# Strassen blocks in three of the four quarters of the mixed group's first product, and residual-only results on ScalarE and GpSimd

## The chip, the cores and the metric

The kernel runs on one core of a Trainium2 chip. Its time is the device time of one execution in microseconds; the time before is the median of three runs. The engines are TensorE (PE in the profile; PEld is its weight load), VectorE (DVE), ScalarE (ACT), GpSimd (POOL) and SyncE (SP, which issues transfers).

## The reference, cut to what matters

Attention with exponential features on both signs, then a normalised two-layer product with a residual:

```python
# attention: batch 8, heads 8, seq 576, head_dim 64, 128 features
def phi(x):
    proj = x @ w_phi; proj = proj - max(abs(proj))
    return concat([exp(proj), exp(-proj)])
kv = phi(k).T @ v ;  z = sum(phi(k));  attn = (phi(q) @ kv) / (phi(q) @ z + 1e-6)
# the rest: 8 x 576 tokens of 512
xn = (x - mean) / sqrt(var + 1e-6) * g_ln
out = x + max(xn @ w_ch1, 0) @ w_ch2        # 512 -> 2048 -> 512
```

All 4608 tokens go through both products. Only these two products, and of them the end, are touched by the change.

## The kernel before, in words

The tokens of the second part are worked in nine groups of 512 (`NM` = 4 tiles of 128 tokens). Groups 0 to 6 are ordinary ones, group 7 (`MIX`) holds the tokens that are left over from every sequence, group 8 (`LAST`) is the last. For a group the first product makes `hT`, 2048 hidden rows in 16 steps `jj` of 128 (`first`, L1425): four matmuls of 512 columns each and a relu. The second product, followed by the residual, makes `o` and stores it. Four steps `jj` are a quarter.

Groups 6, 7 and 8 (`FAST`) do the second product with Strassen's seven products for each pair `p` of token tiles (`fast`, L1541). It has two chains of accumulators, `ch`, and seven results; each is scaled by `rstd` and added to `o`. Four of the seven are "fresh": they are the first to write their piece of `o` and add the residual `x` instead of an older `o`. In group 7 the two chains lie in one tile of two banks, in group 6 and 8 in tiles of their own.

Group 8 does the first product by Strassen as well, group 7 in one quarter of four (`QUICK`, L533). A Strassen quarter (`quick`, L1744) has seven products of four matmuls with 256 columns. They go to three accumulators: name 1 is the single bank `n_bank`, names 0 and 2 are chains that several products are added to. A chain is read between its products: `sum_` on VectorE adds a copy of another chain to it and writes `hT`; `keep` copies a chain to SBUF for a later `sum_`; a relu ends it. The weights' sums (`F`, in the buffers `b_0`, `b_1`, `b_2`, `qkT_141` to `qkT_143` and `v_101`) and the tokens' sums (`X`, in `ea` and `eb`) are made by VectorE before.

The order of all engines is written out when the kernel is built, by a planner (`Order.run`, L365). It takes every operation with an assumed duration and with the keys that it reads and writes, and gives an engine that is free the waiting operation with the lowest rank. An operation that may run on two engines goes to the one that takes it first. `latest` (L374) works due times back from an operation's users. The ranks of the attention come from these. On the chip every engine works its own queue in that order and waits by semaphores, which the framework sets by the tiles that instructions read and write. The planner's keys don't set them.

Of the kernel before, what the change touches and what calls it, by code (L numbers as in the profile page):

```python
# [10 lines left out]
FP32 = mybir.dt.float32  # L11
BF16 = mybir.dt.bfloat16
AF = mybir.ActivationFunctionType
# [283 lines left out]
class Op:  # L297
    __slots__ = (
        "engines", "engine", "us", "emit", "rank", "lag", "deps", "users", "acquire", "release",
        "ready", "left", "number", "due", "load", "cut", "last",  # L300
    )
# [25 lines left out]
class Order:  # L327
# [5 lines left out]

    def add(self, engine, us, rank, emit, r=(), w=(), acquire=None, release=None, lag=None, due=None, load=None, cut=None, last=False):
        op = Op()
        op.last = last
# [28 lines left out]
    def run(self):  # L365
# [23 lines left out]
        while events:  # L389
# [12 lines left out]
            for engine, queue in waiting.items():  # L402
# [54 lines left out]
                elif isinstance(us, Turn):  # L457
                    ahead = backlog["DMA"]
                    if free["DMA_w"] > now:
                        ahead *= 3.4  # L460
                    us = max(us.us, max(0.0, free["DMA"] - now) + ahead - 0.5)
                elif isinstance(us, Op):
                    us = 1.1 if us.engine == "ACT" else 0.0
                if engine == "POOL" and op.load is None:
# [26 lines left out]
def kernel(  # L491
# [40 lines left out]
    FAST = (LAST - 2, LAST - 1, LAST)  # L532
    QUICK = {LAST: range(4), MIX: (2,)}  # L533
    LEAD = 24
    CP = JC // 2
    FH = DM // 2
# [1004 lines left out]
    def fast(g, p, i, cs):  # L1541
# [59 lines left out]

        def result():
# [3 lines left out]
            nc.vector.scalar_tensor_tensor(  # L1606
                out=o, in0=sums(), scalar=rstd_x[:, g, t : t + 1],
# [76 lines left out]
    def sums_of_w1(gate):  # L1684
# [3 lines left out]
        for i in range(2):  # L1688
            for home_ in (b16_home[i], qkT_home[i]):
                add("SP", 0.0, RELU, None, w=[*home_, (home_[0], "free")])  # L1690
        for home_ in (b16_home[2], qkT_home[2], v_home, *U_home, *W_home, *Y_home):
            add("SP", 0.0, RELU, None, w=[*home_, (home_[0], "free")])
        for half in range(2):
# [8 lines left out]
            for i in (0, 1, 3, 2):  # L1702
                a, b, op_, reads = todo[i]

                def emit(k, out_=F_of[half][i], a=block(a), b=block(b), op_=op_):
                    nc.vector.tensor_tensor(out=out_[:, k], in0=a[:, k], in1=b[:, k], op=op_)

                for k in range(2):
                    add("DVE", Port(0.32), 2000.0 + half, lambda k=k, f=emit: f(k),
                        r=[("w1", n_, kc) for n_ in range(2 * half, 2 * half + 2) for kc in range(KC)]  # L1710
                        + [("F", half, j, k) for j in reads] + [(F_at[half][i][1][0], "free"), *gate],
                        w=[("F", half, i, k)])

    def sums_of_x(g):
# [9 lines left out]

        add("SP", 0.0, RELU, None, w=[*X_home[g], ("X home", g)])
        todo = ((X1, block(0, 1), block(0, 0), ()), (X2, block(1, 1), own(X1), (0,)),
                (X3, block(1, 1), block(0, 1), ()), (X4, block(1, 0), own(X2), (1,)))
        for i in range(4):
            out_, a, b, reads = todo[i]

            def emit(k, out_=own(out_), a=a, b=b):
                nc.vector.tensor_tensor(out=out_[:, k], in0=a[:, k], in1=b[:, k], op=ALU.subtract)

            for k in range(2):
                add("DVE", Port(0.2), RELU if g == LAST else 2001.0, lambda k=k, f=emit: f(k),
                    r=[("xT", g % XB, kc) for kc in range(KC)] + [("X", g, j, k) for j in reads]
                    + [("X home", g)], w=[("X", g, i, k)])

# [5 lines left out]
    def quick(g, d):  # L1744
# [26 lines left out]
        def products(name, left, right, start, stop, r, w=(), acquire=None):  # L1771
            def emit():
                if start:
                    st[name] = (
                        n_bank[:, 0 : 2 * FH] if name == 1
                        else ps_B.tile([P, 2 * FH], FP32, tag="B", name="sum")
                    ).rearrange("p (c t) -> p c t", c=2)
# [6 lines left out]

            add("PE", mm(4, FH), turn_of(g), emit, r=r, w=[("quick", g, d, name), *w], acquire=acquire,
                due=due(g, 4 * d / JC) + (0.0 if start and name < 2 else 40.0))
# [21 lines left out]
        def keep(name):  # L1808
            def emit(engine):
                kept(name)  # L1810
                if engine == "DVE":
                    nc.vector.tensor_copy(out=st["kept", name], in_=st[name])
                else:
                    nc.scalar.copy(out=st["kept", name], in_=st[name])
# [14 lines left out]
        X = [[("X", g, i, k) for k in range(2)] for i in range(4)]  # L1829
        def sum_(odd_, t, name, other, w, release=None):  # L1830
            add("DVE", 0.66, RELU,
                both(ring_at(odd_, t), lambda: st[name], lambda: st["kept", other]),
                r=[q_key(name), ("kept", other, d % 2)], w=w, release=release)

        products(1, A(0, 1), B(1, 0), True, True, w_keys + x_keys, acquire=("N", 1))
        yield
        keep(1)
        products(0, A(0, 0), B(0, 0), True, True, w_keys + x_keys, acquire=("B", 1))
        yield
        sum_(0, 0, 0, 1, even)  # L1840
        products(2, S(0), T(0), True, True, F[0] + X[0], acquire=("B", 1))
        yield
# [9 lines left out]
        add(("ACT", "DVE"), (0.55, 0.6), RELU, relu(ring_at(1, 0), lambda: st[0]),  # L1852
            r=[q_key(0)], w=odd, release=("B", 1))
        products(2, S(3), B(1, 1), False, True, F[3] + x_keys)
        yield
        sum_(0, 1, 2, 0, even, release=("B", 1))
# [26 lines left out]
    def moe(g):  # L1883
# [5 lines left out]
        if g == LAST:  # L1889
            quick_moe(g)  # L1890
            return
        quicks = None
        if QUICK.get(g):
            sums_of_w1([("S", p, 2, SH) for p in range(2)])
            sums_of_x(g)
            quicks = quick(g, QUICK[g][0])
        for jj in range(JC):
            if g <= LAST and jj // 4 not in QUICK.get(g, ()):
                if quicks and jj >= JC - 4:
                    for _ in range(2):  # L1900
                        next(quicks, None)
# [202 lines left out]
```

## Time and profile before

| what | value |
|---|---|
| median of 3 runs | 356.84 us (356.49 to 356.98) |
| profiled execution | 356.53 us |
| its span | 354.7 us |
| TensorE busy | 346.6 us (98%) |
| VectorE busy | 302.5 us (85%) |
| ScalarE busy | 257.9 us (73%) |
| GpSimd busy | 196.5 us (55%) |

A row of a group of instructions gives line, engine, operation, tiles written and read, shapes, count, then busy time and mean duration of one in ns, then the idle time before them and who ended it. A row of the timeline gives start, duration, engine, line, operation, tiles and count. A row of the chain of waits gives start and length of a piece of the chain that ended last. Times are counted from the start of the span.

### The profile page before, as it was taken

How to read it: one execution, taken by the hardware profiler on the slowest of the kernel's cores; microseconds unless marked ns; L12 is line 12 of the kernel's file. 1: busy time of each engine (PE TensorE's matmuls, PEld its weight loads, DVE VectorE, ACT ScalarE, POOL GpSimd, SP SyncE). 2: the span in 40 equal slices, each digit the busy share in tenths (PEclk: the TensorE clock that was granted, in tenths of full speed). 3: DMA queues.
4: the chain of work that ended last, by engine and by line, in shares of the span. 5: the costliest groups of instructions: out<-in, count | busy, mean ns of one | idle time of the engine just before them, and what ended most of it. 6: DMA issues, size and time to landing. Idle time of an engine off the chain costs nothing.

```text
span 354.7 us, 9383 instructions
## 1 busy us (share of the span) xinstructions
PE 346.6 (98%) x3615; PEld 221.7 (62%) x3640; DVE 302.5 (85%) x659; ACT 257.9 (73%) x553; POOL 196.5 (55%) x249
## 2 busy tenths in 40 slices
PE   8999999999999999999999999999999999999995
PEld 8988855556554555454545555555555578578884
DVE  5699989799998888878889899887778799999983
ACT  4998977598988897969696875887697833656410
POOL 5389756596765876648579698565546411000000
PEclk9999999999999999999999999999999999999999
DMA  8999999999997878389629542851051004500053
GB/s 212 325 197 269 205 260 270 243 245 239 292 250 205 208 184 224 104 168 252 201 69 178 103 110 41 150 156 35 2 126 63 3 9 115 124 0 3 0 120 118
DMA packets 93676, 53.89 MB, mean 152 GB/s; under 512 B 61104, under 2 KB 88048, under 8 KB 93632
## 3 DMA queue, kind: packets, MB, share of 16 engines
q1 hardware_dynamic: 89392, 47.72, 56.3%
q0 software_dynamic: 3328, 4.49, 7.4%
q10 hardware_dynamic: 912, 1.08, 1.0%
q8 instruction: 28, 0.46, 0.5%
q14 instruction: 16, 0.13, 0.1%
HBM read 36.77 MB, written 9.44 MB: 130 GB/s over the span
## 4 chain that ended last, share of the span: by engine, by line
PE 87%; DVE 7%; ACT 4%; issue 1%; POOL 0%; DVEq 0%
PE hT_ps L1431 29%; PE ch_ps L1463 23%; PE ch L1597 9%; PE pm L990 4%; PE n_bank L1141 4%; PE sum L1780 4%; PE num L1199 3%; PE n_bank L2064 3%; ACT ea L1111 2%; PE pt L999 2%; PE n_bank L1135 1%; DVE numc L1221 1%; DVE m L1047 1%; DVE numc L1227 1%; PE n_bank L1199 1%
## 5 line engine op out<-in xcount | busy, mean ns | idle before, releaser
L1431 PE MATMUL hT_ps<-xT,w 128*128 128x512 bf16 x496 | 119.5, 379 | 0.1
L1463 PE MATMUL ch_ps<-w,hT 128*128 128x512 bf16 x363 | 89.3, 379 | 1.3 <-issue 0.3
L1047 DVE TENSOR_REDUCE m<-pm 128x8 f32<-128x1024 f32 x64 | 77.0, 1216 | 8.1 <-PE pm L990 6.4
L1074 POOL TENSOR_TENSOR vv<-v,ek 128x1024 bf16<-128x1024 f32 x32 | 61.0, 1907 | 37.9 <-issue 21.3
L1431 PEld LDWEIGHTS <-w 128*128 128x128 bf16 x496 | 43.9, 98 | 43.2 <-issue 1.3
L1067 ACT ACTIVATE eb<-pm 128x1024 bf16<-128x1024 f32 x64 | 65.0, 1039 | 4.4 <-DVE m L1047 4.4
L1111 ACT ACTIVATE ea<-pt 128x1024 bf16<-128x1024 f32 x64 | 64.1, 1039 | 3.5 <-PE pt L999 2.7
L1441 ACT ACTIVATE hT<-hT_ps 128x512 bf16<-128x512 f32 x73 | 43.7, 599 | 24.9 <-PE hT_ps L1431 24.1
L1266 POOL TENSOR_TENSOR x<-numc,rden 128x128 bf16<-128x128 f32 (+1 forms) x64 | 39.1, 614 | 39.9 <-DVE rden L1233 37.9
L1463 PEld LDWEIGHTS <-hT 128*128 128x128 bf16 x384 | 34.0, 98 | 34.3 <-issue 0.8
L1439 DVE TENSOR_SCALAR hT<-hT_ps 128x512 bf16<-128x512 f32 x51 | 34.8, 685 | 8.4 <-PE hT_ps L1431 8.0
L1199 PEld LDWEIGHTS <-ea 128*128 128x128 bf16 x512 | 24.6, 97 | 9.9 <-issue 0.7
L902 POOL TENSOR_TENSOR b<-qk,one 128x1024 bf16<-128x1024 f32 x14 | 26.9, 1927 | 4.7 <-DMA qkT<-b 3.0
L1141 PE MATMUL n_bank<-vv,eb 128*128 128x65 bf16 x512 | 26.7, 194 | 0.0
L2064 PE MATMUL n_bank<-wz 128*128 128x120 bf16 x355 | 25.5, 226 | 0.1
L1141 PEld LDWEIGHTS <-eb 128*128 128x128 bf16 x512 | 22.3, 98 | 4.5
L1338 DVE BATCH_NORM_STATS2 st<-x 128x6 f32<-128x512 bf16 (+1 forms) x40 | 21.8, 572 | 1.7 <-POOL x L1266 1.4
L2064 PEld LDWEIGHTS <-wz 128*128 128x128 bf16 x355 | 22.2, 104 | 1.1
L1480 POOL TENSOR_TENSOR o<-o,x 128x512 f32<-128x512 f32 x15 | 17.4, 1157 | 10.1 <-ACT o L1476 9.9
L1221 DVE TENSOR_TENSOR numc<-num,em 128x390 f32<-128x390 f32 (+1 forms) x40 | 20.4, 515 | 2.7 <-PE num L1205 1.6
L1227 DVE TENSOR_TENSOR numc<-numc,num 128x390 f32<-128x390 f32 (+1 forms) x40 | 20.5, 517 | 0.5
L1476 ACT ACTIVATE o<-ch_ps,rstd 128x512 f32<-128x512 f32 x15 | 10.3, 686 | 14.3 <-PE ch_ps L1463 14.3
(162 smaller groups left out, 618.4 us busy)
## 6 DMA issues: line engine op xcount, KB each, us to landing
out_dram<-o SPq DMA_DIRECT2D x29, 256.0 KB, 2.4
qk<-in_k_dram SPq DMA_DIRECT2D x12, 512.0 KB, 5.4
qk<-in_q_dram SPq DMA_DIRECT2D x12, 512.0 KB, 6.4
v<-in_v_dram SPq DMA_DIRECT2D x12, 512.0 KB, 4.7
w<-in_moe_w_ch_dram POOLq DMA_DIRECT2D x4, 1024.0 KB, 11.3
qk<-in_k_dram SPq DMA_DIRECT2D x8, 256.0 KB, 6.8
qk<-in_q_dram SPq DMA_DIRECT2D x7, 256.0 KB, 7.1
v<-in_v_dram SPq DMA_DIRECT2D x7, 256.0 KB, 7.6
```

What stands on the lines that cost most here:

```text
L1047: nc.vector.reduce_max(out=m, in_=ps, axis=AX.X, apply_absolute_value=True)
L1067: nc.scalar.activation(eb, ps, AF.Exp, scale=(1.0, -1.0)[t])
L1074: eng.tensor_tensor(out=u["vv"][:, :, 0:MX, 0:D], in0=bcast(vb[:, hh, :].rearrange("p (c d) -> p c d", d=D), 1, 2), in1=bcast(e[:, :, 0:MX ...
L1111: nc.scalar.activation(u["EA"][:, t, 0:1024], u["pt"], AF.Exp, scale=(1.0, -1.0)[t])
L1141: nc.tensor.matmul(ps[:, t, c // 4, :], EB[:, t, c, :], vv[:, t, c, :], start=False, stop=(t == 0 and c == MX - 1), skip_group_check=True,)
L1199: nc.tensor.matmul(ps[t][:, i, :], ea(u, t, c), KV[:, t, c // 4, :], start=True, stop=True,)
L1266: eng.tensor_tensor(out=dst, in0=src, in1=by, op=ALU.mult)
L1431: nc.tensor.matmul(st["ps"], w1_sb[:, kc, jj * P : (jj + 1) * P], xT_bufs[g % XB][:, kc::KC, :], start=(kc == 0), stop=(kc == KC - 1),)
L1439: nc.vector.tensor_relu(h_sb, st["ps"])
L1441: nc.scalar.activation(h_sb, st["ps"], AF.Relu)
L1463: nc.tensor.matmul(ch[g, i], hT[g, jj][:, i * P : (i + 1) * P], w2_sb[:, jj, :], start=(jj == 0), stop=(jj == JC - 1),)
L2064: nc.tensor.matmul(warm, wz, wz[:, 0:WN], start=False, stop=False, skip_group_check=True)
```

## The change

`QUICK` gives group 7 quarters 1, 2 and 3 to Strassen in place of quarter 2 alone. The two chains of such a quarter, names 0 and 2, no longer take a bank each from the pool `ps_B`. They share one tile of two banks, `sum2`, from `ps_A`. All three quarters are put to the planner at their own place, in place of one that was spread over the last steps. The copies and two of the closing relus, which could go to VectorE or ScalarE, are ScalarE's alone. A fresh result of groups 6 and 7 may go to ScalarE, which scales it into `o`; GpSimd then adds the residual. Users marked `calm` no longer count when due times are worked back. What is computed stays the same.

```diff
-    QUICK = {LAST: range(4), MIX: (2,)}
+    QUICK = {LAST: range(4), MIX: (1, 2, 3)}
+    EITHER = lambda g, i: g != LAST
...
-            late = min((latest[o.number] for o in op.users), default=1000.0) - op.lag
+            late = min((latest[o.number] for o in op.users if not o.calm), default=1000.0) - op.lag
...
# fast(): results
+            if engine == "ACT":
+                nc.scalar.activation(o, sums(), AF.Copy, scale=rstd_x[:, g, t : t + 1])
+                return
...
-        add("DVE", 0.44, RELU, result, r=[("fast", g, p, bank)],
-            w=o_key + ([counts["slot", g, t]] if i in (0, 3) else []),
-            release=gave)
+        either = fresh and EITHER(g, i)
+        op = add(
+            ("DVE", "ACT") if either else ("DVE",), (0.44, 0.46)[: 1 + either], RELU,
+            result if either else lambda: result("DVE"), r=[("fast", g, p, bank)], w=w, release=gave,
+        )
+        if either:
+            def residual():
+                if op.engine == "ACT":
+                    o = ch["o", g, t][:, f]
+                    nc.gpsimd.tensor_tensor(
+                        out=o, in0=o, in1=token_tile(g, t)[2][:, f], op=ALU.add
+                    )
+            add("POOL", op, RELU, residual, r=[], w=o_key, cut=0.6)
...
# quick(): the chains
+                    if g == MIX and name == 0:
+                        st["A"] = ps_A.tile([P, 2, 2 * FH], FP32, tag="A", name="sum2")
                     st[name] = (
                         n_bank[:, 0 : 2 * FH] if name == 1
+                        else st["A"][:, name // 2, :] if g == MIX
                         else ps_B.tile([P, 2 * FH], FP32, tag="B", name="sum")
...
-            add(("ACT", "DVE"), (0.55, 0.6), RELU, emit, r=[q_key(name), (home_, "free")],
-                w=[("kept", name, d % 2)], release=("N", 1) if name == 1 else None)
+            add("ACT", 0.55, RELU, emit, r=[q_key(name), (home_, "free")],
+                w=[("kept", name, d % 2)], calm=True, release=("N", 1) if name == 1 else None)
...
-        add(("ACT", "DVE"), (0.95, Port(0.4)), RELU, relu(wide_, lambda: wide_), w=even)
-        add(("ACT", "DVE"), (0.55, Port(0.25)), RELU, relu(ring_at(1, 1), lambda: ring_at(1, 1)), w=odd)
+        add("ACT", 0.95, RELU, lambda f=relu(wide_, lambda: wide_): f("ACT"), w=even, calm=True)
+        add("ACT", 0.55, RELU, lambda f=relu(ring_at(1, 1), lambda: ring_at(1, 1)): f("ACT"), w=odd, calm=True)
...
# moe(): where the quarters are put to the planner
-            quicks = quick(g, QUICK[g][0])
...
+                for _ in quick(g, jj // 4):
+                    pass
```

The order is the same on every engine up to about the start of group 7's first product. Three places differ in what matters here. In the rows below `sum_5505`, `sum_5514` and `sum_5633` are the two-bank tiles of quarters 1, 2 and 3 of group 7 and `sum` is a chain in a bank of its own; `xT_139` are group 7's tokens and `xT_140` group 8's; what stands in brackets are the engines whose semaphores a row waits for. Of a product's four matmuls the first is shown.

First, TensorE at the start of Strassen's products in group 7. Before:

```order
L1780 MATMUL n_bank<-xT_139,w_132 128x256
...
L1780 MATMUL sum<-xT_139,w_132 128x256 [waits Activation_49]
...
L1431 MATMUL hT_ps<-xT_139,w_132 128x512 [waits Activation_49]
...
L1780 MATMUL sum<-ea_125,qkT_141 128x256 [waits Activation_49]
...
L1597 MATMUL ch_5556<-w_133,hT 128x256
...
L1780 MATMUL sum<-ea_125,qkT_142 128x256 [waits DVE_49]
...
L1780 MATMUL sum<-xT_139,qkT_143 128x256 [waits DVE_49]
```

Now:

```order
L1803 MATMUL n_bank<-xT_139,w_132 128x256
...
L1803 MATMUL sum_5505<-xT_139,w_132 128x256 [waits DVE_49]
...
L1803 MATMUL sum_5514<-xT_139,w_132 128x256
...
L1803 MATMUL sum_5505<-ea_125,b_0_145 128x256 [waits DVE_49]
...
L1803 MATMUL n_bank<-xT_139,w_132 128x256 [waits Activation_49]
...
L1803 MATMUL sum_5514<-ea_125,qkT_141 128x256
...
L1803 MATMUL sum_5505<-ea_125,b_1_146 128x256 [waits Activation_49]
...
L1803 MATMUL sum_5505<-xT_139,b_2_147 128x256
...
L1803 MATMUL n_bank<-xT_139,w_132 128x256 [waits Activation_49]
...
L1803 MATMUL sum_5514<-xT_139,qkT_143 128x256 [waits DVE_49]
```

and ScalarE and VectorE with it, now (ScalarE's rows first):

```order
L1834 COPY kept<-n_bank 128x512 [waits PE_49]
L1834 COPY vx_107<-sum_5505 128x512 [waits DVE_49]
L1834 COPY kept<-n_bank 128x512 [waits PE_49]
L1834 COPY vx_106<-sum_5514 128x512 [waits PE_49]
L1834 COPY qx_89<-sum_5505 128x512 [waits PE_49]
...
L1820 TENSOR_TENSOR hT<-sum_5505,kept 128x2x256 [waits PE_49,Activation_49]
L1752 TENSOR_TENSOR eb_148<-xT_139,ea_125 128x256 [waits DVE_49] x2
L1820 TENSOR_TENSOR hT<-sum_5514,kept 128x2x256 [waits Activation_49]
```

Before, wide matmuls of `hT_ps` and products of `ch` stood between the products of one quarter; now products of two quarters alternate, each with its two chains in one tile.

Second, TensorE in quarter 3 of group 7, which before was worked in wide matmuls of `hT_ps`. Now:

```order
L1803 MATMUL sum_5633<-xT_139,w_132 128x256 [waits DVE_49]
...
L1803 MATMUL sum_5633<-ea_125,qkT_141 128x256
...
L1600 MATMUL ch_5645<-w_133,hT 128x256 [waits PE_49]
...
L1803 MATMUL sum_5633<-ea_125,qkT_142 128x256 [waits DVE_49]
...
L1803 MATMUL sum_5633<-xT_139,qkT_143 128x256 [waits Activation_49]
...
L1803 MATMUL sum<-ea_127,v_101 128x256 [waits Activation_49]
...
L1803 MATMUL sum_5633<-ea_125,v_101 128x256 [waits Activation_49]
...
L1803 MATMUL sum<-eb_149,w_132 128x256 [waits DVE_49]
L1803 MATMUL sum_5633<-eb_148,w_132 128x256 [waits DVE_49]
```

Three products of this quarter now wait, one of them directly behind a product that it shares the tile with.

Third, VectorE around 295 us, with the results of group 6 (`o<-ch`) and the first weight sums. Before:

```order
L1233 RECIPROCAL rden<-numc 128x6
L1706 TENSOR_TENSOR b_0_145<-w_132 128x512
L1606 SCALAR_TENSOR_TENSOR o<-ch_5291,rstd,x 128x256
L1706 TENSOR_TENSOR b_0_145<-w_132 128x512
L1606 SCALAR_TENSOR_TENSOR o<-ch_5303,rstd,x 128x256
L1606 SCALAR_TENSOR_TENSOR o<-ch_5282,rstd,o 128x256
L1338 BN_STATS st<-x 128x6
```

Now, and behind the dots the end of GpSimd's queue:

```order
L1236 RECIPROCAL rden<-numc 128x6
L1612 SCALAR_TENSOR_TENSOR o<-ch_5303,rstd,o 128x256
L1725 TENSOR_TENSOR b_0_145<-w_132 128x512 x2
L1341 BN_STATS st<-x 128x6 x2
L1612 SCALAR_TENSOR_TENSOR o<-ch_5282,rstd,o 128x256
...
L1269 TENSOR_TENSOR x<-numc,rden 128x2x3x64
L1646 TENSOR_TENSOR o<-o,x 128x256 x2
L1269 TENSOR_TENSOR x<-numc,rden 128x2x3x64
L1646 TENSOR_TENSOR o<-o,x 128x256 x5
L1646 TENSOR_TENSOR o<-o,xm 128x256 x7
```

Fourteen of the sixteen fresh results of groups 6 and 7 left VectorE; the weight sums moved up, and fourteen adds stand at the end of GpSimd's queue.

More of the change, by code (lines that the diff above doesn't have):

```diff
@@ L299 @@
         "engines", "engine", "us", "emit", "rank", "lag", "deps", "users", "acquire", "release",
-        "ready", "left", "number", "due", "load", "cut", "last",
+        "ready", "left", "number", "due", "load", "cut", "last", "calm",
     )
@@ L462, in run @@
                 elif isinstance(us, Op):
-                    us = 1.1 if us.engine == "ACT" else 0.0
+                    us = (op.cut or 1.1) if us.engine == "ACT" else 0.0
                 if engine == "POOL" and op.load is None:
@@ L1600, in products, with result @@
                 )
-        def result():
+        def result(engine):
             if i in (0, 3):
@@ L1783, in emit @@
                         )
-            add("PE", mm(4, FH), turn_of(g), emit, r=r, w=[("quick", g, d, name), *w], acquire=acquire,
+            add("PE", mm(4, FH), turn_of(g), emit, calm=not (start and name < 2), r=r, w=[("quick", g, d, name), *w], acquire=acquire,
                 due=due(g, 4 * d / JC) + (0.0 if start and name < 2 else 40.0))
@@ L1808, in keep, with emit @@
         def keep(name):
-            def emit(engine):
+            def emit():
                 kept(name)
[L1811 to L1814, printed above, removed]
+                nc.scalar.copy(out=st["kept", name], in_=st[name])
             home_ = (U_home, Y_home, W_home)[name][d % 2][0]
-            add(("ACT", "DVE"), (0.55, 0.6), RELU, emit, r=[q_key(name), (home_, "free")],
-                w=[("kept", name, d % 2)], release=("N", 1) if name == 1 else None)
+            add("ACT", 0.55, RELU, emit, r=[q_key(name), (home_, "free")],
+                w=[("kept", name, d % 2)], calm=True, release=("N", 1) if name == 1 else None)
         def relu(out_, in_):
@@ L1891, in moe @@
             return
-        quicks = None
         if QUICK.get(g):
-            sums_of_w1([("S", p, 2, SH) for p in range(2)])
+            sums_of_w1([("S", p, 0, SH) for p in range(2)])
             sums_of_x(g)
-            quicks = quick(g, QUICK[g][0])
         for jj in range(JC):
             if g <= LAST and jj // 4 not in QUICK.get(g, ()):
-                if quicks and jj >= JC - 4:
-                    for _ in range(2):
-                        next(quicks, None)
                 first(g, jj)
```

44 lines of the change are left out of this document (25 added, 19 removed).

## The prediction

> **What bounds the kernel now.** I read the shares first, then the tail of the program in slices of ten microseconds, then the waits of TensorE, then the chain of waits.
>
> ```profile
> span 354.7 us, 9383 instructions
> PE 346.6 (98%) x3615; PEld 221.7 (62%) x3640; DVE 302.5 (85%) x659; ACT 257.9 (73%) x553; POOL 196.5 (55%) x249
> ...
> 290.00:300.00 10.00, 9.77 (x90) 8.62 (x89) 9.98 (x29) 2.37 (x5) 0.90 (x1) 1.00 0.29 54
> 300.00:310.00 10.00, 10.00 (x59) 5.49 (x58) 9.31 (x31) 6.43 (x13) 0.00 (x0) 1.00 0.59 159
> 310.00:320.00 10.00, 10.00 (x82) 7.83 (x80) 9.71 (x27) 5.73 (x11) 0.00 (x0) 1.00 0.00 0
> 320.00:330.00 10.00, 10.00 (x94) 8.96 (x92) 8.59 (x20) 6.08 (x10) 0.00 (x0) 1.00 0.01 2
> ...
> PE ch L1597 <- DVE o L1606: 0.2, 1, 0.2
> PE ch_ps L1463 <- issue: 0.2, 1, 0.2
> ...
> 292.83 8.02 PE ch L1597 x72
> 300.86 6.91 PE hT_ps L1431 x32
> ...
> 337.85 13.11 PE ch L1597 x120
> 350.96 0.03 issue
> ```
>
> The columns of the slices are stretch, length, then busy time of TensorE, weight loads, VectorE, ScalarE and GpSimd, and the granted clock (1.00). After 240 us TensorE waits 0.4 us in all, and from 292.83 to 350.96 it runs without a gap. So the end of the program is TensorE's work in this stretch, plus whatever it waits; the 3.7 us behind 350.96 (last result, store) do not change. VectorE is at 9.98, 9.31 and 9.71 of 10 us in the stretch that the change rewrites: it bounds nothing yet, but has little slack. ScalarE and GpSimd are light there. The order on every engine is the same up to about 290 us, so only what follows counts.
>
> **Work taken from TensorE.** 32 matmuls of 512 columns take 6.91 us, 0.216 each; 120 of 256 columns take 13.11 us, 0.109 each. A plain quarter has 16 of the former, 3.46 us, a Strassen quarter 28 of the latter, 3.06 us (seven products of four, 0.437 each). Two more quarters: **-0.79 us**. The sums of weights and tokens that Strassen needs were made before too, so they add nothing.
>
> The 0.2 us that TensorE waits for `o` at 292.8 belongs to a result which now goes to ScalarE, idle there: **-0.20** (bounds -0.35, with the refill below, and 0).
>
> **Waits put into TensorE's queue.** Before, each Strassen chain had its own bank; now both chains of a MIX quarter lie in one tile, and the order shows the waits. ScalarE's copy of the second half (`vx_107<-sum_5505`) waits for VectorE, though TensorE wrote that half; and the next product into the first half (`sum_5505<-ea_125,b_1_146`) waits for ScalarE, though VectorE read that half. So sum and copy, which could run side by side, stand behind one another, with TensorE behind both. Their prices:
>
> ```profile
> L1797 DVE TENSOR_TENSOR hT<-sum,kept 128x512 bf16<-128x512 f32 x3 | 2.1, 686 | 0.1
> L1814 ACT COPY vx<-sum 128x512 f32<-128x512 f32 x3 | 1.8, 585 | 0.2 <-PE sum L1780 0.2
> ...
> 317.54 0.68 DVE L1797 TENSOR_TENSOR hT<-sum,kept 128x512 bf16<-128x512 f32 x1
> 318.28 0.59 ACT L1814 COPY qx<-sum 128x512 f32<-128x512 f32 x1 [1.50 <-DVE hT L1797]
> 332.71 0.58 ACT L1814 COPY vx<-sum 128x512 f32<-128x512 f32 x1
> 333.19 0.59 ACT L1814 COPY qx<-sum 128x512 f32<-128x512 f32 x1
> ```
>
> A sum takes 0.69, a copy 0.59; copies in a row start 0.49 apart (332.71, 333.19); from VectorE's end (317.54 + 0.68) to ScalarE's start 0.06, so I take 0.05 for each hand-over. When TensorE starts again it loses about 0.15: the 72 matmuls after the gap at 292.83 took 8.02 us, against 72 x 0.109 = 7.87.
>
> Place 1, quarter 1 of MIX. Count from the end of its `n_bank` product. Its copy `kept` ends at 0.69 (0.05, about 0.05 behind the last relu, 0.59). TensorE makes three products, to 1.31; the third writes the second half of `sum_5505`, and VectorE's sum waits for that too: 1.36 to 2.05. The copy `vx_107` follows, 2.10 to 2.69, and TensorE may go on at 2.74. In between it has two products, to 2.19: **0.55 us of waiting**.
> Place 2, quarter 2. ScalarE starts its next two copies at 2.59 and 3.08 and ends the latter, `vx_106`, at 3.67; the sum of `sum_5514` runs 3.72 to 4.41; TensorE needs it at 4.46. It came on at 2.74, lost 0.15, and did three products, to 4.20: **0.26**.
> Place 3, quarter 3. Count from the end of the first sum of `sum_5633`. TensorE makes `sum_5633<-ea_125,qkT_142`, 0.05 to 0.49; the copy `vx_107` comes behind this write, 0.54 to 1.13; and directly behind in TensorE's queue stands `sum_5633<-xT_139,qkT_143`, which waits for the copy, to 1.18: **0.69**.
> Place 4, same quarter. That product ends at 1.18 + 0.15 + 0.44 = 1.77, the copy `qx_89` at 2.41, TensorE goes on at 2.46; one product in between, to 2.21: **0.25**.
> Together 1.75, and four refills, 0.60: **+2.35**. In the other quarters, the last group's, each chain keeps its own bank. Two rows of the same kind stand further on (`sum_5633<-eb_148` and a `sum<-eb_149`, both behind a sum of VectorE): 0 to 0.69 each; I take 0.05 each and the refills, **+0.40**, nearer to nothing since other products stand ahead of them.
> For the four the bounds are 0 (if the waits named are met early) and 3.4 (four sums of 0.69 in full, four refills).
>
> **Results on ScalarE and GpSimd.** Seven residual-only results of group 6 and seven of MIX leave VectorE, and GpSimd adds the residual.
>
> ```profile
> L1606 DVE SCALAR_TENSOR_TENSOR o<-ch,rstd,x 128x256 f32<-128x256 f32 x16 | 7.7, 479 | 1.7 <-PE ch L1597 1.6
> L1476 ACT ACTIVATE o<-ch_ps,rstd 128x512 f32<-128x512 f32 x15 | 10.3, 686 | 14.3 <-PE ch_ps L1463 14.3
> L1480 POOL TENSOR_TENSOR o<-o,x 128x512 f32<-128x512 f32 x15 | 17.4, 1157 | 10.1 <-ACT o L1476 9.9
> ...
> L956 ACT ACTIVATE eb<-n_bank 128x128 bf16<-128x128 f32 x10 | 2.9, 285 | 0.2
> ...
> L1355 DVE TENSOR_SCALAR xc<-x,mv 128x512 bf16<-128x512 bf16 x1 | 0.3, 350 | 0.0
> ...
> 291.92 0.88 DVE o L1606 x2
> 305.85 0.48 DVE L1732 TENSOR_TENSOR ea<-xT 128x256 bf16<-128x256 bf16 x2
> ```
>
> No row has the new shapes. For ScalarE's half-width result I take 0.43, between 0.29 (128 columns) and 0.69 (512); for GpSimd's add 0.58, half of 1.157. Both engines have room for them: from 290 to 300 ScalarE is idle 7.6 us of 10, GpSimd 9.1. VectorE is freed of 7 x 0.4 = 2.8 us before 305 (two results take 0.88 from start to end, about 0.4 apart), less 0.3 for a centring that comes to it from ScalarE. The first token sum, which ended at 306.33, could end at 303.8. TensorE now needs it early, after 16 wide matmuls and three products: 300.86 - 0.20 + 3.46 + 1.31 = 305.4. That leaves a cover of 1.6 us.
>
> The cover is eaten by GpSimd:
>
> ```profile
> 295.17 0.39 DVE L1706 TENSOR_TENSOR b<-w 128x512 bf16<-128x512 bf16 x1
> 295.34 0.90 POOL L1266 TENSOR_TENSOR x<-numc,rden 128x384 bf16<-128x384 f32 x1 [6.15 <-DVE rden L1233]
> 295.47 0.48 DVE L1606 SCALAR_TENSOR_TENSOR o<-ch,rstd,x 128x256 f32<-128x256 f32 x1
> 295.87 0.65 DVE L1706 TENSOR_TENSOR b<-w 128x512 bf16<-128x512 bf16 x1
> ...
> 206.50 2.12 POOL L1512 TENSOR_TENSOR qk<-w 128x1024 bf16<-128x1024 bf16 x1
> 207.38 1.79 DVE L1512 TENSOR_TENSOR qk<-w 128x1024 bf16<-128x1024 bf16 x1
> ```
>
> A weight sum on VectorE takes 0.39 alone and 0.65 with GpSimd at work, 0.26 more; at 207.38 one ends 0.55 after GpSimd's end, as if it had only started there. The result that reads the accumulator (295.47) is not slowed. Seven adds before 303 at 0.26 cost VectorE 1.8 us: 0.2 more than the cover, with a refill **+0.35**. The bounds are 0 (they fall beside other work) and 2.6 (seven at the full 0.58, less the cover, plus refill).
>
> The Trainium skill (SBUF — State Buffer, "Who interferes with whom") says that a VectorE instruction with two inputs in SBUF and a GpSimd instruction that reads SBUF exclude each other, and that the later one blocks to the end of the first. The rows at 206.50 agree, the one at 295.87 a little less, since 0.37 us of GpSimd's instruction were left there. What full blocking would give here stands in the third rival, from rows.
>
> **Sum.** -0.79 - 0.20 + 2.35 + 0.40 + 0.35 = +2.11. On the profiled execution (356.53, span 354.7) that gives 358.6 and a span of 356.8; the median shown, 356.84, lies 0.31 higher, so 359.0.
>
> **Rivals.**
> 1. Faster. The order names an engine to wait for, not an instruction. If the waits at the places are for earlier work, already done, copy and sum run side by side: place 1 would be ready at 2.00, before TensorE's 2.19, and the others likewise. Then 356.84 - 0.79 - 0.20 = 355.85. It decides once TensorE's work between two uses of a tile is longer than one link (0.69). Against it: the copy's only wait is for VectorE, which wrote nothing that this copy reads.
> 2. Half of the waits. If the queue of TensorE runs behind VectorE's by a product or so, places 2 and 4 and the two small ones vanish (0.51 + 0.30 + 0.40 = 1.2): 357.7. For it: the small places are within 0.3 of being covered.
> 3. Full blocking by GpSimd. About half of VectorE's time there is two-input sums, so five of seven adds meet one, and each costs 0.5: 2.5, less the cover 1.6, plus refill, +1.05 in place of 0.35: 359.7. For it: 206.50. Against it: 295.87.
> 4. No difference. TensorE loses only at place 3 (0.69 + 0.15), the rest is covered: -0.99 + 0.84 gives 356.7.
>
> **Chances.** Forecast 0.50 (358.2 to 359.6), rival 1 0.09, rival 2 0.17, rival 3 0.14, rival 4 0.10. The kernel's runs tell a change from none at about 0.2%, 0.7 us; so faster 0.09, same 0.10, slower 0.81. The range 357.5 to 360.3 leaves out rivals 1 and 4; above 360.3 most of GpSimd's and the waits' upper bounds would have to come together.
>
> **What would show it.** Right: TensorE's waits after 300 us rise from nothing to some 2 us, on rows of `sum`, put down to ScalarE's copies and VectorE's sums, four of them 0.2 to 0.8 long; matmul time falls by 0.8; weight sums near GpSimd's adds last about 0.6. Wrong: TensorE still without a gap from 293 to the end, which is rival 1 and a faster kernel; or one long wait at the first token sum (rival 3).

## The result and the profile after

| what | before | after |
|---|---|---|
| median | 356.88 us (356.49 to 356.98) | 358.99 us (358.66 to 359.41) |
| ratio | 1 | 1.0063, interval 1.0049 to 1.0077 |
| profiled execution | 356.53 us | 359.41 us |
| its span | 354.7 us | 357.4 us |

The kernel became slower by 2.1 us, 0.63%. The shares on the page show nothing of it:

```profile
span 357.4 us, 9462 instructions
PE 346.8 (97%) x3639; PEld 223.5 (63%) x3664; DVE 301.9 (84%) x648; ACT 267.5 (75%) x574; POOL 211.6 (59%) x263
```

TensorE's busy time even rises by 0.2, though its matmuls cost 0.79 less: a matmul's row goes on for a while after the next one could have started (0.16 us, see below), so part of what TensorE loses at a wait counts as busy. The tail in slices of ten microseconds shows more (TensorE, weight load, VectorE, ScalarE, GpSimd, clock, then the DMA share and GB/s):

```profile
290.00:300.00 10.00, 9.86 (x91) 8.68 (x90) 10.00 (x27) 4.34 (x10) 4.41 (x6) 1.00 0.29 54
300.00:310.00 10.00, 9.17 (x68) 6.40 (x66) 8.56 (x29) 7.21 (x15) 6.23 (x2) 1.00 0.59 159
310.00:320.00 10.00, 9.15 (x82) 7.73 (x81) 8.76 (x22) 7.32 (x12) 0.00 (x0) 1.00 0.00 0
...
330.00:340.00 10.00, 9.75 (x90) 8.56 (x88) 9.15 (x23) 6.26 (x11) 2.33 (x3) 1.00 0.07 15
```

Where TensorE had 10.00 of 10 between 300 and 320, it now has 9.17 and 9.15, at the same clock of 1.00. VectorE and ScalarE have slack there, so no engine is full: they wait for one another. TensorE's waits from 286 us on name the rows:

```profile
PE sum L1803 <- ACT vx L1834: 1.3, 2, 0.7
PE sum L1803 <- DVE late L1820: 0.3, 1, 0.3
PE sum L1803 <- DVE hT L1820: 0.2, 1, 0.2
PE sum L1803 <- ACT qx L1834: 0.2, 1, 0.2
```

And the chain of waits, which before was TensorE's from 292.83 to 350.96, now leaves it for VectorE and ScalarE:

```profile
293.96 7.15 PE ch L1600 x64
301.11 3.45 PE hT_ps L1434 x16
...
306.41 0.70 DVE hT L1820
...
307.14 0.59 ACT vx L1834
307.72 0.49 ACT kept L1834
308.21 0.50 ACT vx L1834
...
308.73 0.70 DVE hT L1820
...
309.48 1.47 PE sum L1803 x12
...
318.24 0.61 PE sum L1803 x4
...
318.87 0.59 ACT qx L1834
...
319.51 0.60 PE sum L1803 x4
...
341.40 12.24 PE ch L1600 x112
```

This is the chain that the prediction described: sum, then copies, then sum, with TensorE behind them.

**How small differences are read here.** The times of one kernel differ by more than most of the terms. Up to about 290 us the order is the same on every engine, in all kernels below. (TensorE's is the same to 304 us, behind the start of group 7's first product; VectorE's, ScalarE's and GpSimd's part at about 291.) So beside each time stands the *stretch*: from the start of group 6's 32 matmuls to the end of TensorE's last one.

```profile
288.03 3.69 PE L1597 MATMUL ch<-w,hT 128*128 128x256 bf16 x32
```

That is the row before. With 350.96 the stretch is 62.93 us. After:

```profile
288.38 3.69 PE L1600 MATMUL ch<-w,hT 128*128 128x256 bf16 x32
```

With 341.40 + 12.24 = 353.64 it is 65.26 us, 2.33 longer. A *gap* is what TensorE loses between two rows: from start to start, less 0.109 us for each matmul of 256 columns. The *wait* of a row is shorter. The profile counts it from the end of the matmul before, and by the profile that matmul lasts 0.27 us, 0.16 longer than the 0.109 after which the next can start (a row of four lasts 0.60, three starts and 0.27). The 0.16 that a gap has beyond its wait is what the prediction calls the refill.

A stretch is read from one execution, the profiled one. The medians of the spans of all executions, each against the kernel before in the same series, go the same way, if not always as far: own banks -0.25, no residual add +1.7, results on VectorE +2.4, own banks in one quarter +1.9, planner told +2.0, the last two of the next table -0.5 and -0.65. One execution of the run with results on VectorE took 1616 us at full clock; its cause is not known, and the ratio leaves it out.

### The profile page after: what moved, and what is told of

It reads as the page before. It is cut to its first block, busy times and chain, and to the rows that moved or that the text cites. A ratio compares the mean times of both kernels' runs of the same rounds, so it can differ in the third digit from the quotient of the medians.

```text
span 357.4 us, 9462 instructions
## 1 busy us (share of the span) xinstructions
PE 346.8 (97%) x3639; PEld 223.5 (63%) x3664; DVE 301.9 (84%) x648; ACT 267.5 (75%) x574; POOL 211.6 (59%) x263
## 4 chain that ended last, share of the span: by engine, by line
PE 81%; DVE 12%; ACT 4%; issue 2%; POOL 0%; DVEq 0%
PE hT_ps L1434 24%; PE ch_ps L1466 23%; PE ch L1600 9%; PE sum L1803 5%; PE pm L993 4%; PE n_bank L2082 3%; PE n_bank L1144 3%; PE num L1202 3%; PE pt L1002 2%; DVE numc L1224 2%; ACT ea L1114 2%; DVE m L1050 2%; DVE hT L1442 1%; DVE numc L1230 1%; PE n_bank L1138 1%
## 5 line engine op out<-in xcount | busy, mean ns | idle before, releaser
L1434 PE MATMUL hT_ps<-xT,w 128*128 128x512 bf16 x464 | 112.1, 379 | 0.6 <-DVE hT L1442 0.6
L1434 PEld LDWEIGHTS <-w 128*128 128x128 bf16 x464 | 40.8, 98 | 40.6 <-issue 1.9
L1444 ACT ACTIVATE hT<-hT_ps 128x512 bf16<-128x512 f32 x65 | 39.0, 600 | 22.9 <-PE hT_ps L1434 22.1
L1646 POOL TENSOR_TENSOR o<-o,xm 128x256 f32<-128x256 f32 x7 | 5.1, 731 | 29.9 <-DVE hT L1820 19.4
```

Source lines behind the costliest of these rows:

```text
L1434: nc.tensor.matmul(st["ps"], w1_sb[:, kc, jj * P : (jj + 1) * P], xT_bufs[g % XB][:, kc::KC, :], start=(kc == 0), stop=(kc == KC - 1),)
L1444: nc.scalar.activation(h_sb, st["ps"], AF.Relu)
```

## The experiments

Theory A is the prediction's: the shared tile makes sum and copy wait for each other. Rival B: GpSimd's adds hold VectorE up. Rival C: three Strassen quarters in a row are too many, whatever the tile. Rival D came later: the planner's order is at fault. The ratios are to the kernel before, with 95% intervals.

| run | stretch | against 62.93 | ratio |
|---|---|---|---|
| the change | 65.26 | +2.33 | 1.0063 (1.0049 to 1.0077) |
| own banks | 62.87 | -0.06 | 0.9991 (0.9978 to 1.0003) |
| no residual add | 64.96 | +2.03 | 1.0055 (1.0037 to 1.0073) |
| results on VectorE | 66.26 | +3.33 | 1.0092 (1.0065 to 1.0120) |
| before, with shared results | 62.88 | -0.05 | 0.9993 (0.9980 to 1.0006) |
| own banks, results on VectorE | 64.17 | +1.24 | 1.0050 (1.0035 to 1.0066) |
| own banks, no add | 62.56 | -0.37 | 0.9997 (0.9975 to 1.0019) |
| own banks, two quarters | 62.75 | -0.18 | 1.0011 (0.9992 to 1.0031) |
| shared tile, two quarters | 64.42 | +1.49 | 1.0045 (1.0030 to 1.0059) |
| own banks in one quarter | 64.88 | +1.95 | 1.0048 (1.0026 to 1.0070) |
| planner told | 65.72 | +2.79 | 1.0073 (1.0048 to 1.0097) |
| two quarters, few results | 62.44 | -0.49 | 0.9990 (0.9977 to 1.0003) |
| three quarters, few results | 62.40 | -0.53 | 0.9999 (0.9983 to 1.0015) |

**Own banks.** The second chain of a quarter of group 7 comes from `ps_B`, and each chain gives its room back by itself; otherwise the change as it is.

```diff
-                        else st["A"][:, name // 2, :] if g == MIX
+                        else st["A"][:, 0, :] if g == MIX and name == 0
...
-        over = [("over", g, d)] if g == MIX else []
+        over = []
...
```

> The change with one thing altered: in group 7's three Strassen quarters the second chain lies in a bank of its own, so that no tile has two chains. The order of group 7's and group 8's products shifts a little with it; the work is the same. Theory A (the shared tile makes sum and copy wait for each other, with TensorE behind both): the four waits of 0.59, 0.23, 0.70 and 0.20 us and their refills, 2.3 us in all, go, and the time falls from 359.0 to 356.7, between 356.3 and 357.4; no wait of TensorE on a row of `sum` over 0.3 stays but perhaps one at the first token sum. Rival B (GpSimd's adds hold VectorE up, and the waits only show it): the adds stay, so the waits stay on VectorE's sums, 358.5 to 359.2. Rival C (three Strassen quarters in a row are more than VectorE and ScalarE can serve, whatever the tile): the waits move to other rows with the same sum, 358.3 to 359.2.

The stretch falls by 2.39 us, and TensorE has no wait on any row of `sum`. The planner's order moves with the edit, though: from 307.4 on TensorE takes a product of quarter 3 earlier, and eleven results instead of fourteen go to ScalarE. The run with own banks in one quarter holds the order fixed. The timeline of this kernel shows what the bank alters:

```profile
306.37 0.68 DVE L1820 TENSOR_TENSOR hT<-sum,kept 128x512 bf16<-128x512 f32 x1
306.68 0.59 ACT L1834 COPY vx<-sum 128x512 f32<-128x512 f32 x1 [0.67 <-PE sum L1803]
...
307.79 0.60 PE L1803 MATMUL sum<-ea,b 128*128 128x256 bf16 x4
```

Sum and copy lie ahead of the first difference in order. The copy starts 0.31 into the sum and waited for TensorE. With the shared tile the same two stand in a row:

```profile
306.41 0.69 DVE L1820 TENSOR_TENSOR hT<-sum,kept 128x512 bf16<-128x512 f32 x1 [0.31 <-PE sum L1803]
...
307.14 0.59 ACT L1834 COPY vx<-sum 128x512 f32<-128x512 f32 x1 [1.47 <-DVE hT L1820]
307.77 0.60 PE L1803 MATMUL sum<-ea,b 128*128 128x256 bf16 x4 [0.59 <-ACT vx L1834]
```

B and C expected the waits to stay or to move, and neither happened. But the kernel is not faster than before either, though its matmuls cost 0.79 less. What eats that is small gaps: 0.30 at 294.30, four of 0.09 to 0.16 between 312 and 321, and 0.29 at 324.78, where group 7's second product follows a result of ScalarE and one of VectorE. With a last one of 0.04 they come to 1.11, against 0.39 before: -0.79 + 1.11 - 0.39 = -0.07, and -0.06 was measured.

**No residual add.** The residual of ScalarE's fourteen results is left out.

```diff
-                if op.engine == "ACT":
+                if False:
```

> The change without GpSimd's adds: the residual of the fourteen results that ScalarE makes is left out, the order is the same on every engine. Theory A: the four waits on the shared tiles stay; only the wait at 293.96 (0.3 us with its refill 0.45) and a little of what VectorE loses later falls away, 358.99 - 0.5 = 358.5, between 358.2 and 358.9. Rival B (the adds hold VectorE up and so make the waits): the four waits go or shrink, 357.3 or less. If nothing falls at all, 358.9 or more, the adds cost nothing.

The order is the same on the four other engines. The four waits on the tiles keep their size (0.60, 0.23, 0.67, 0.18), so B falls. The stretch is 0.30 shorter, a little less than expected; the median, 359.41, lies above the range that A gave, and in the time the difference can't be told from nothing. What the add did is seen on VectorE, first without it, then in the change:

```profile
292.32 0.40 DVE L1537 TENSOR_TENSOR qk<-hT,qk 128x512 bf16<-128x512 bf16 x1
...
293.69 1.04 PE L1600 MATMUL ch<-qk,qk 128*128 128x256 bf16 x8
```

```profile
292.23 0.67 POOL L1646 TENSOR_TENSOR o<-o,x 128x256 f32<-128x256 f32 x1 [0.15 <-ACT o L1610]
...
292.37 0.81 DVE L1537 TENSOR_TENSOR qk<-hT,qk 128x512 bf16<-128x512 bf16 x1
...
293.96 1.03 PE L1600 MATMUL ch<-qk,qk 128*128 128x256 bf16 x8
```

One sum that starts under an add takes 0.81 in place of 0.40, the result behind it comes later, and TensorE has a gap of 0.30 at 293.96. Without the add there is none.

**Results on VectorE.**

```diff
-            if engine == "ACT":
+            if engine == "ACT" and False:
...
-                if op.engine == "ACT":
+                if False:
```

> The change with the fourteen results made by VectorE again, with their residual, at the same places of the order; ScalarE's results and GpSimd's adds are gone. Theory A: the four waits stay at their size; VectorE has 7 x 0.4 = 2.8 us more to do before 305, its first token sum comes later by more than the cover of 1.6, so TensorE waits there 0.5 to 1.2 more: 359.3 to 360.2, slower than the change. Rival B (GpSimd's adds are what costs): faster than the change by the lock, 357.5 to 358.5.

The stretch is 1.00 longer than the change's, where A expected 0.3 to 1.2, and the tile's waits stay (0.67, 0.23, 0.67, 0.18). The new one is at the first token sum:

```profile
305.65 0.49 DVE L1752 TENSOR_TENSOR ea<-xT 128x256 bf16<-128x256 bf16 x2
305.99 0.69 PE L1803 MATMUL sum<-ea,b 128*128 128x256 bf16 x4 [0.37 <-DVE ea L1752]
```

With the refill and a late second matmul that is 0.6 of the 1.0; two gaps at 292.58 and 293.71, where TensorE waits for results, lose 0.3 more than the one at 293.96 in the change. The median without the execution of 1616 us, 360.54, lies a little above A's range. So with three quarters the sharing of results is worth 1.0 us by the stretch: it has VectorE ready in time.

**Before, with shared results.** `result` and `residual` of the change in the kernel before, one Strassen quarter, chains in their own banks.

```diff
-                    us = 1.1 if us.engine == "ACT" else 0.0
+                    us = (op.cut or 1.1) if us.engine == "ACT" else 0.0
...
+    EITHER = lambda g, i: g != LAST
...
```

> The kernel before with the second part of the change alone: residual-only results may go to ScalarE, GpSimd adds the residual; one Strassen quarter in group 7, its chains in banks of their own. Theory A: nearly nothing, since TensorE has no other wait there; the 0.2 us at 292.8 with its refill may go or may come back at 293.9 as in the change: 356.4 to 357.0 beside 356.88. Rival B: VectorE, which has little slack before the first token sum, is held up by the adds, and TensorE waits: 357.3 to 358.3.

Nothing, as A said (0.9993 of 356.88 is 356.6, within its range). The gap of 0.39 at 292.83 goes, and one of 0.30 comes at 294.64, as in the change.

**Own banks, results on VectorE.** Both edits together.

> Own banks for the chains, and the fourteen results made by VectorE again at the same places of the order, as in the run with results on VectorE. Theory A (tile and results are two separate costs): the waits on the tile are gone as with own banks, the results cost what they cost there, 1.0 us: 357.6, between 357.1 and 358.4, relative to 357.0 of own banks. Rival B (what own banks gave came from VectorE having time to spare): with VectorE full again most of the 2.5 us come back, 358.5 or more.

In the time A missed: the median is 358.67, above its 358.4 and inside what B expected. The stretch speaks for A. It is 1.30 longer than with own banks, not most of 2.5. The tile is worth 66.26 - 64.17 = 2.09 us here, with no result on ScalarE, and 2.39 with shared results, so it is a cost of its own. But the results cost 1.30, not 1.0. The rest is mostly a place that I had not counted:

```profile
326.14 0.47 DVE L1612 SCALAR_TENSOR_TENSOR o<-ch,rstd,xm 128x256 f32<-128x256 f32 x1
...
326.67 0.60 PE L1600 MATMUL ch<-w,hT 128*128 128x256 bf16 x4 [0.54 <-DVE o L1612]
```

A result of group 7 stands late in VectorE's queue. Group 7's two chains lie in one tile as well; whether that adds to this wait was not tried.

**Own banks, no add.** The residual of ScalarE's results is left out.

> Own banks, and GpSimd's adds left out: the residual of the results that ScalarE makes is missing. This shows where the 0.79 us of matmul time went that own banks did not bring. Theory A: the wait at 294 (0.30 with its refill) goes, the small gaps further on (0.1 to 0.3 each, 0.8 in all) stay: 356.7, between 356.4 and 357.0. Rival B: the small gaps are GpSimd's doing too and go: 356.0 or less.

The stretch is 0.31 shorter: the gap at 294 goes, those of 0.09 to 0.29 from 312 on stay. They are not GpSimd's. The time itself is too uncertain to say anything.

**Own banks, two quarters.** With the edit of own banks:

```diff
-    QUICK = {LAST: range(4), MIX: (1, 2, 3)}
+    QUICK = {LAST: range(4), MIX: (1, 2)}
...
```

> Own banks, with Strassen in quarters 1 and 2 of group 7 and quarter 3 plain: 0.40 us more matmul time than with three, against fewer small gaps. Theory A (each gap comes from VectorE having to serve the chains one after the other; fewer quarters leave it slack): 356.7, between 356.2 and 357.1. Rival C (three quarters do not bind anything): 0.4 slower than own banks, 357.4.

The stretch is 0.12 shorter than with three, although the matmuls cost 0.40 more: from 296 on one gap is left, 0.32 at 333.40. So the third quarter brings in gaps what it saves in matmuls. In that weak form C of the list above is right; the rival of this run, 0.4 slower, is not.

**Shared tile, two quarters.**

```diff
-    QUICK = {LAST: range(4), MIX: (1, 2, 3)}
+    QUICK = {LAST: range(4), MIX: (2, 3)}
```

> The change with two of its three quarters: 2 and 3 by Strassen, each with its chains in one tile; quarter 1 is plain again, 0.40 us more matmul time. Theory A: the waits come with each quarter that shares a tile; two quarters should have some 1.0 to 1.4 us of waits and refills against 2.3, less 0.39 saved beside the kernel before: 357.7, between 357.3 and 358.3. Rival C (three in a row are too many, whatever the tile): two are fine, 356.9 or less.

C's number is far off, and so is A's (358.65). The tile's two gaps, 0.32 and 0.39, come to 0.7, less than the 1.0 to 1.4 that A gave to waits and refills of the tile. The largest gap, 0.58, is not on the tile: its product reads `b`, as none does in quarters 2 and 3 of group 7, so it is group 8's, whose chains have banks of their own.

```profile
322.92 0.61 PE L1803 MATMUL sum<-ea,b 128*128 128x256 bf16 x4 [0.43 <-DVE hT L1820]
```

It waits for a sum of VectorE. I had left it out, with 0.15 behind it, the 0.30 of GpSimd's add and a gap of 0.36 where group 7's second product waits for ScalarE's result.

**Own banks in one quarter.** Each engine's order is exactly the change's.

```diff
-                        else st["A"][:, name // 2, :] if g == MIX
+                        else st["A"][:, name // 2, :] if g == MIX and (own == 0 or name == 2 * (own - 1))
...
```

Here `own` is 2 in quarter 1 (the first chain comes from `ps_B`) and 0 in the others.

> The change with every engine's order left exactly as it is; only in quarter 1 of group 7 the first chain lies in a bank of its own, so that sum and copy of this quarter are in different tiles. Theory A (the tile makes the waits, not the order): the waits of place 1 (0.59, with refill 0.75) and, since its cause lies in TensorE's late restart and ScalarE's row of copies, most of place 2 (0.23, with refill 0.40) go, places 3 and 4 stay at 0.67 and 0.18; something of up to 0.5 comes back where the bank is taken over by a later chain. In the stretch from group 6's second product to TensorE's last matmul 65.26 falls to 64.3 to 64.9. Rival D (own banks won because the planner's order changed with it): nothing changes at place 1, 65.2 to 65.4.

Place 1's gap of 0.75 is gone with no instruction moved, which settles tile against order there. Sum and copy overlap again, and TensorE goes on without a wait:

```profile
306.72 0.68 DVE L1821 TENSOR_TENSOR hT<-sum,kept 128x512 bf16<-128x512 f32 x1
...
307.04 0.59 ACT L1835 COPY vx<-sum 128x512 f32<-128x512 f32 x1 [0.67 <-PE sum L1804]
...
307.71 0.60 PE L1804 MATMUL sum<-ea,b 128*128 128x256 bf16 x4
```

Place 2 stays at 0.19, and a wait of 0.25 comes in at 313.72, where a chain of group 8 takes over the bank and waits for ScalarE's relu of the chain that held it; places 3 and 4 are untouched:

```profile
PE sum L1804 <- ACT vx L1835: 0.7, 1, 0.7
...
PE sum L1804 <- ACT hT L1846: 0.2, 1, 0.2
PE sum L1804 <- DVE hT L1821: 0.2, 1, 0.2
PE sum L1804 <- ACT qx L1835: 0.2, 1, 0.2
```

That place 2 would mostly go was wrong: there VectorE's sum follows ScalarE's copies of its own tile, whenever TensorE came on.

**Planner told.** Products, sums and copies of a shared tile all write the key `over`, so the planner puts them one behind another.

```diff
-                w=[("kept", name, d % 2)], calm=True
+                w=[("kept", name, d % 2), *(over if name != 1 else [])], calm=True
...
-        products(0, S(1), T(1), False, True, F[1] + X[1])
+        products(0, S(1), T(1), False, True, F[1] + X[1], w=over)
...
-                r=[q_key(name), ("kept", other, d % 2), *r], w=w, release=release, calm=True)
+                r=[q_key(name), ("kept", other, d % 2)], w=w + over, release=release, calm=True)
```

> The change with its shared tiles, but the planner is told that products, sums and copies of one tile follow one another, so that it can put other products of TensorE between them. Theory A (the links are a chain of 0.69 + 0.59 per use that three quarters in a row cannot hide): the waits change place but keep their sum within 0.7 us, 358.3 to 359.9 beside 359.0 of the change. Rival D (the planner's order is at fault, because it took the two halves for independent): most of the 2.3 us go, 357.3 or less.

Not better, rather worse (65.72). The waits lie elsewhere, mostly behind VectorE:

```profile
PE sum L1803 <- DVE hT L1820: 1.1, 3, 0.4
PE sum L1803 <- ACT qx L1834: 0.2, 1, 0.2
```

This order knows of the links and pays no less for them, so D falls, as far as one other order can tell.

**Two and three quarters, few results.** Own banks; of group 6's results only some may leave VectorE.

```diff
-    QUICK = {LAST: range(4), MIX: (1, 2, 3)}
+    QUICK = {LAST: range(4), MIX: (1, 2)}
...
-    EITHER = lambda g, i: g != LAST
+    EITHER = lambda g, i: g == LAST - 1 or g == LAST - 2 and i in (0,)
...
```

With three quarters the set is `(0, 6)`.

> An attempt at a version below both kernels: own banks, Strassen in quarters 1 and 2 of group 7, and of group 6's residual-only results only the first of each pair may go to ScalarE (six results on ScalarE and GpSimd in all, in place of eleven to fourteen). Theory A (what is left to win is the matmul time of one more quarter, 0.40, and the wait of 0.39 at 293, less what the add of GpSimd brings back there, 0.30): the stretch from group 6's second product to TensorE's last matmul, 62.93 before, should come to 62.4 to 62.8, the time to 356.3 to 356.8 beside 356.9: too little to tell from no change. Rival C (anything more on ScalarE's and GpSimd's side or in a row of quarters costs): 357.2 or more.

> The same with all three quarters, and of group 6's residual-only results the first and the last of each pair on ScalarE (nine in all). Theory A: 0.79 less matmul time than before, and of the gaps of own banks (1.1 us) those behind VectorE shrink, as it has fewer adds of GpSimd to collide with: the stretch 62.2 to 62.8, the time 356.2 to 356.8. Rival C: the gaps stay as with own banks, 62.8 to 63.1, 356.7 to 357.2.

Both stretches are where A put them, 0.5 us under the kernel before. In the time neither can be told from no change (the second's 357.0 even lies where C put it), so no version here is shown to beat the kernel before.

## Why the prediction was right, step by step

Time, sign and main mechanism were right (359.0 forecast, 358.99 measured). That they agree to a hundredth is luck: the four executions lie 0.75 apart, one step failed, and two terms came out by other ways than forecast.

1. **TensorE bounds the tail:** right. The chain ends in 12.24 us of its matmuls, and the 3.7 us behind them did not change (357.4 - 353.64 = 3.8).
2. **-0.79 of matmul time:** right. Sixteen wide matmuls are left, 3.45 us (301.11), and three narrow products take 1.47 (309.48), with the 0.16 by which the last matmul's row outlasts the next one's start, so 0.437 each, as priced.
3. **Four waits on the shared tile, 1.75 and four refills of 0.15:** right, place by place. Place 1 waited 0.59 (forecast 0.55), place 2 0.23 (0.26), place 3 0.67 (0.69), place 4 0.18 (0.25):

```profile
309.48 0.60 PE L1803 MATMUL sum<-xT,qkT 128*128 128x256 bf16 x4 [0.23 <-DVE hT L1820]
...
318.24 0.60 PE L1803 MATMUL sum<-xT,qkT 128*128 128x256 bf16 x4 [0.67 <-ACT vx L1834]
...
319.51 0.60 PE L1803 MATMUL sum<-ea,v 128*128 128x256 bf16 x4 [0.18 <-ACT qx L1834]
```

With refills the gaps are 0.75, 0.40, 0.83 and 0.34, together 2.32 against 2.35. For place 1 it is shown, with nothing moved, that the tile makes the wait (own banks in one quarter). Places 2 to 4 go with own banks too, but there the order moved with the edit, so for them it is likely and not shown. Why two engines that only read a tile are put in a row was read from the order and not tried.

The size of a refill was right, its reading was not. In the kernel before, the chain's row of 72 matmuls that took 8.02 us runs to the end of the last one. The matmul behind them starts earlier:

```profile
300.69 7.07 PE L1431 MATMUL hT_ps<-xT,w 128*128 128x512 bf16 x32
```

That is 7.86 after 292.83, 0.109 for each of the 72, so TensorE lost nothing behind that gap. A wait costs 0.16 more than itself because it begins at a matmul's end.

4. **Two small rows, +0.40:** near in size by luck. The two products that the order showed start at 320.87 (`sum<-eb_149`), with no gap, and at 321.45 (`sum_5633<-eb_148`), with a gap of 0.13 and no wait named. The rest is a wait that the prediction did not name, 0.25 and a refill, at a later product of group 8. It follows a sum into `late`, which holds hidden rows of group 8 alone, and group 8's chains share no tile:

```profile
330.72 0.60 PE L1803 MATMUL sum<-eb,w 128*128 128x256 bf16 x4 [0.25 <-DVE late L1820]
```

5. **"The cover is eaten by GpSimd", +0.35, and -0.20 for the old wait:** this step failed. I took one row, a weight sum of 0.65 beside a GpSimd instruction, for all seven adds. Only two places were slowed by more than 0.1: 0.41 at 292.37, and 0.46 at 294.68 (1.71 for two sums, 1.25 without the adds). The long run of weight sums was not slowed at all. Without the adds and in the change its last pair reads:

```profile
303.56 0.76 DVE L1725 TENSOR_TENSOR v<-w 128x512 bf16<-128x512 bf16 x2
```

```profile
301.02 6.23 POOL L1646 TENSOR_TENSOR o<-o,x 128x256 f32<-128x256 f32 x2 [3.48 <-ACT o L1610]
...
304.13 0.75 DVE L1725 TENSOR_TENSOR v<-w 128x512 bf16<-128x512 bf16 x2
```

Counted from the start of the stretch, the first token sum comes 16.42 us in, and 15.83 without the adds: they cost VectorE 0.59 there, not 1.8, and TensorE did not wait for it. The cover was smaller than forecast as well: without the adds the pair of token sums ends 0.7 before TensorE's product starts, not 1.6, and in the change 0.4 before. The price was paid at 293.96 in place of 292.83: 0.39 went, 0.30 came. Together these two terms gave -0.09 where I had +0.15.

6. **The sum.** By these gaps -0.79 + 2.32 + 0.54 - 0.09 = +1.98. The remaining 0.35 of the stretch's +2.33 is mostly five rows that lost 0.05 to 0.07 each with no wait named (0.28), which I had not priced. So +2.11 was close partly because a term too large stood for one that was missing, and because group 8's wait of step 4 stood for two that hardly came.
7. **Rivals.** The first is refuted by TensorE's four waits, and by the copy that starts as the sum ends. The second needed places 2 and 4 and the two small rows to vanish; the places are there, and only the small rows nearly vanished. The third needed a long wait at the first token sum; there is none. The fourth needed all but place 3 covered.

## What to carry to other kernels

Look at what a semaphore sees, not at which bytes are touched: two accumulation chains in one tile made independent readers wait for each other, and TensorE behind both, for 2.1 to 2.4 us here, some three times the matmul time that the change saved. Price such a link as reader, hand-over, reader, and set it against the products that TensorE has in between. Where they were too few here, a bank each gained those 2.1 to 2.4 us, and the one order that knew of the links gained nothing. And when a saving is below what the time can tell, read it on a stretch whose start is common to all kernels.

## What the runs showed of the hardware

**Who waits for whom, VectorE or GpSimd, goes by who is already there.** A lone sum that started under an add took 0.81, not 0.40, and ended 0.28 after the add. But in a run of fourteen weight sums without a break VectorE lost nothing (0.75 and 0.76 for two, with and without adds), and it was GpSimd that stood: two adds took 6.23 us where one takes 0.67, so the first took about 5.6. It started at 301.02, within the run, and ended at about 306.6, half a microsecond after the six token sums that follow the run without a break (306.10). The Trainium skill (SBUF — State Buffer, "Who interferes with whom") says that the later of the two blocks to the end of the first. The first row roughly agrees (0.28 is less than a whole sum). The second goes further: the add was held not for one instruction of VectorE but for the whole back-to-back run.

**TensorE's refill is overlap that a wait takes away.** Gap less wait was 0.16, 0.17, 0.16, 0.16 and 0.16 at the five waits of the change. By the profile, whose ends of matmuls are modelled, it has to be: a matmul of 256 columns lasts 0.27 us and the next one can start 0.109 after it. Two rows behind such waits, at 318.73 and 320.00, started another 0.05 late with no wait named.

**The part that no kernel altered varied more than the change cost.** The start of the stretch lay between 287.83 and 290.29 us. The two latest starts show other waits earlier on, one for VectorE, one for a load:

```profile
PE n_bank L946 <- DVE numc L1230: 1.5, 1, 1.5
```

```profile
PE qkT_ps L832 <- DMA qk<-in_k_dram: 1.6, 1, 1.6
```

The first is the shared tile with two quarters, the second two quarters with few results. Neither wait is in the other kernel's profile, nor in that of the change.
